# A fused Fourier-mixing and hard-swish kernel: weight conversions of the first block split into halves and reordered

## The chip, the cores and the metric

The kernel runs on one core of a Trainium2 chip. A core has five instruction streams that matter here: PE (TensorE, the matrix engine; "PEld" in the profile is its loading of weights, which overlaps its products), DVE (VectorE), ACT (ScalarE), POOL (GpSimd) and SP (SyncE, which here only issues DMAs). Each stream runs its instructions in the order in which they are written, and waits where a semaphore says that data or a buffer is not ready.

The metric is the device time of one execution in microseconds (us). Before the change the median of four runs is 2700.55 us.

## The reference

```python
def _attn_ref(x, filt_r, filt_i):          # x: 8 x 3008 x 256
    X = np.fft.rfft(x, axis=1)
    F = (filt_r + 1j * filt_i)[None, :, :]
    Y = X * F
    y = np.fft.irfft(Y, n=x.shape[1], axis=1)
    return y.astype(np.float32)
...
def _moe_ref(x, w_in, w_out):              # x: 24064 x 256, w_in: 256 x 2048, w_out: 2048 x 256
    h = x @ w_in
    relu6 = np.clip(h + 3.0, 0.0, 6.0)
    g = h * relu6 / 6.0
    return (g @ w_out).astype(np.float32)
```

A sequence of 3008 positions is filtered in the frequency domain, for 8 batches and 256 channels. The 24064 filtered tokens then go through a two-layer network with 2048 hidden units. The two weight matrices come in as 64-bit floats.

## The kernel before

**Blocks and steps.** The network is computed in 47 blocks of 512 tokens. A block takes 8 steps, one for each 256 of the 2048 hidden units (`NP` = 8). With `items` the program counts steps through all blocks: step 8k + p works on block k and hidden part p. In a step PE computes the "up" product (tokens times `w_in[p]`), ACT and DVE make the hard-swish of it, and in the following step PE computes the "down" product (hidden units times `w_out[p]`). Block 0 does this plainly (`plain_up`, L658; `plain_down`, L669): 512-wide products into two PSUM tiles `al` and `be`, then for each of them a `relu` on ACT (L616) and a `hswish` on DVE (L621). `al` can be written again when L621 has read it. From block 1 on (step 8), the products are done with fewer multiplications in a Strassen-like scheme (`up_1` to `up_5`, L571, and `down`, L647), which needs sums of weight blocks beside the weights themselves. These are made once by POOL (`w_sums`, L299): four for each of the 16 weight tiles, three early ones and a "late" one that overwrites a weight block which block 0 still needs.

**The Fourier work** runs between these steps. A function `at(step, fn, ...)` puts a call into a plan; calls of `a_unit`, `b_unit`, `bi_unit` and `n_unit` run early in their step, between the up and the down product, all others run at its end. In the first ten steps the plan has the following. `n_unit` turns transformed data into the tokens of block 1 and 2 (PE L525, ACT L531), after which `t_sums` makes token sums on POOL (L564). `a_unit(1, c)` is the first transform of batch 1, for chunk c in step c + 2: products into two PSUM banks (PE L385), each evicted by ACT (L388). For later batches the second bank goes through DVE (`a_sums`). `z_store` writes the result to DRAM, `x_load` fetches the next chunk, `table_load` the filter tables `ft0` and `ft1`, `t4_load` inputs of `n_unit`, `t2_load` reads the stored chunks back for `b_unit` (PE L437). For batch 1 all of these are issued by SP.

**The weights.** Each of the 16 weight tiles (up 0, down 0, up 1, down 1, ..., up 7, down 7) is loaded as raw 64-bit words (`w_load`, L260) and converted to 32 bits on DVE by seven instructions (`w_conv`, L275 to L293). ACT makes one operand, the magnitude of the upper word (`w_abs`, L266). The first four tiles are converted before block 0. The other twelve are converted by `convert_one` at the end of steps 0, 1, 1, 2, 2, 3, 3, 4, 4, 5, 5, 6, in the order up 2, down 2, up 3, down 3 and so on. `load_bits` asks for the next tile once the tile two places earlier in the same kind of buffer has been converted, so the order on SP's queue depends on where it is called. The sums on POOL are planned from step 6: first the early ones of up 7 and down 7, then stage p in step p + 6.

Of the kernel before, what the change touches and what calls it, by code (L numbers as in the profile page):

```python
# [38 lines left out]
NB = HC // XC  # L39
# [6 lines left out]
NP = DFF // 256  # L46
# [90 lines left out]
def kernel(  # L137
# [9 lines left out]
    nc = tc.nc  # L147
# [47 lines left out]
    st = {}  # L195
# [35 lines left out]

    NCONV = 16

    def w_part(i):
        p = i // 2
        if i % 2 == 0:
            cols = ts(p, 256)
            src = moe_w_in[:, cols].bitcast(I32)
            return src.rearrange("(a p) d -> p a d", p=P), w_in[p][:, 0:4, :].rearrange("p (a j) m -> p a (j m)", a=2)
        src = moe_w_out[ts(p, 2 * P), :].bitcast(I32)  # L240
        return src.rearrange("(a p) d -> p a d", p=P), w_out[p][:, 0:4, :].rearrange("p (a j) m -> p a (j m)", a=2)
# [21 lines left out]
    def w_abs(i):  # L263
        words = st["bits", i].rearrange("p (n two) -> p n two", two=2)
        st["high", i] = sp.tile([P, 512], FP32, name="s1")
        nc.scalar.activation(out=st["high", i], in_=words[:, :, 1].bitcast(FP32), func=AXT.Abs)  # L266


    def w_conv(i):
        words = st.pop(("bits", i)).rearrange("p (n two) -> p n two", two=2)  # L270
        lo, hi = words[:, :, 0], words[:, :, 1]
        big, rest = (yp.tile([P, 2, D], FP32, name="y").bitcast(I32).rearrange("p a n -> p (a n)") for j in range(2))
        v = nc.vector
        high = st.pop(("high", i), None)
        v.tensor_scalar(out=big, in0=hi, scalar1=3, scalar2=0x3FFFFFFF,  # L275
                        op0=ALU.logical_shift_left, op1=ALU.bitwise_and)
        v.scalar_tensor_tensor(out=big, in0=hi, scalar=top_c, in1=big,  # L277
                               op0=ALU.bitwise_and, op1=ALU.bitwise_or)
        v.tensor_scalar(out=rest, in0=big, scalar1=23, scalar2=23,
                        op0=ALU.logical_shift_right, op1=ALU.logical_shift_left)  # L280
        v.tensor_scalar(out=lo, in0=lo, scalar1=9, scalar2=0x3F800000,
                        op0=ALU.logical_shift_right, op1=ALU.bitwise_or)
        if high is None:
            v.tensor_scalar(out=hi, in0=hi, scalar1=1, scalar2=1,
                            op0=ALU.logical_shift_left, op1=ALU.logical_shift_right)
            high = hi.bitcast(FP32)
        rest, big = rest.bitcast(FP32), big.bitcast(FP32)
        v.scalar_tensor_tensor(out=rest, in0=lo.bitcast(FP32), scalar=1.0, in1=rest,  # L288
                               op0=ALU.subtract, op1=ALU.mult)
        v.scalar_tensor_tensor(out=rest, in0=rest, scalar=2.0 ** -20, in1=big, op0=ALU.mult, op1=ALU.add)  # L290

        two = lambda t: t.rearrange("p (a d) -> p a d", a=2)
        v.scalar_tensor_tensor(out=w_part(i)[1], in0=two(high), scalar=1.125 * 2.0 ** -15, in1=two(rest),  # L293
                               op0=ALU.is_ge, op1=ALU.mult)
# [74 lines left out]
    def bank(b):  # L369
        if b:  # L370
            return psF.tile([P, 512], FP32, name="psf", tag="f")
        st["bank"] = i = (st.get("bank", -1) + 1) % 4
        return psO.tile([P, 2, 2, P], FP32, name="po%d" % i).rearrange("p a u m -> p (a u m)")
# [4 lines left out]
    def a_unit(b, c):  # L378
        xc = xs[:, (b * NB + c) % 3, :, :]
        t = t1p.tile([P, XC // 2, 2, D], FP32, name="t1")  # L380
        ps = [bank(b).rearrange("p (j d) -> p j d", d=D) for h in range(2)]
        for j in range(2):
            for g in range(2):
                for h in range(2):
                    nc.tensor.matmul(ps[h][ts(g, 64), j, :], wa[ds(h * 64, NA), ds((c * XC + 2 * g + j) * 2 * KH, 64)],  # L385
                                     xc[ds(h * 64, NA), 2 * g + j, :], start=True, stop=True)
        for h in range(2 if b == 1 else 1):
            nc.scalar.activation(out=t[:, :, h, :], in_=ps[h], func=AXT.Copy)  # L388
        st["t1", b, c] = t, ps[1]


    def a_sums(b, c):
        t, ps = st["t1", b, c]
        nc.vector.tensor_tensor(out=t[:, :, 1, :], in0=t[:, :, 0, :], in1=ps, op=ALU.subtract)
        nc.vector.tensor_tensor(out=t[:, :, 0, :], in0=t[:, :, 0, :], in1=ps, op=ALU.add)  # L395

# [100 lines left out]
    for b in range(B):  # L497
        j = 0
        while j < HC:
            n = 1 if b == 0 and j == NJ else min(NJ, HC - j)  # L500
# [229 lines left out]


    EARLY = (a_unit, b_unit, bi_unit, n_unit)

    def at(step, fn, *a):
        plan.setdefault((step, fn in EARLY), []).append((fn, a))

    with tc.manual_schedule():
# [16 lines left out]
        def load_bits(most):  # L754
            nonlocal loaded
            while loaded < most and w_before(loaded) < done:
                w_load(loaded, nc.sync)
                loaded += 1

        def convert(n):  # L760
            nonlocal done
            for i in range(n):
                w_conv(done)
                done += 1


        def convert_one():
            nonlocal done
            w_abs(done)
            w_conv(done)  # L770
            done += 1
            load_bits(NCONV)

# [2 lines left out]
        ps = psU.tile([P, 512], FP32, name="al")  # L776
# [12 lines left out]
        for j in range(0, HC, 4):  # L789
            a0_unit(j)  # L790
            keep_warm({4: 2, 12: 2, 20: 1}.get(j, 0))
            convert(j == 4)
# [34 lines left out]
        for c in range(2):  # L827
            x_load(1, c)
            load_bits(7 + c)
        w_abs(3)  # L830
        convert(3)

        def wai_load():
# [3 lines left out]
        at(0, bi_unit, 0, NU - 2)  # L837
        at(0, g_store, 0, NU - 2)

        for i, s in enumerate((0, 1, 1, 2, 2, 3, 3, 4, 4, 5, 5, 6)):  # L840
            at(s, convert_one)

        for i in range(2):
            at(6, w_sums, 2 * NP - 2 + i, False)
        for p in range(NP):
            for i in range(2):
                if p < NP - 1:
                    at(p + 6, w_sums, 2 * p + i, False)
                at(p + 6, w_sums, 2 * p + i, True)

        at(0, wai_load)
        at(2, x_load, 1, 2)
# [31 lines left out]
        def places(n):  # L884
            if n == 1:
                return (list(range(2, NB + 2)), [12, 13, 15, 18, 19, 20, 22, 23, 26, 27, 28, 30],
                        [14, 15, 16, 19, 21, 22, 24, 25, 27, 29, 30, 31], [16, 21, 24, 29, 31, 32])
            k = first[n] * NP
            a_at = [k - 7 * NP + i for i in (2, 4, 7, 9, 11, 13, 14, 15)]
            f_at, y_at, bi_at = ([k - (5 - 2 * r) * NP + i for r in range(2) for i in p]  # L890
                                 for p in ((2, 3, 6, 7, 12, 13), (4, 5, 10, 11, 14, 15), (8, 14, 17)))
            return a_at, f_at, y_at, bi_at

        prev = None
        for n in range(1, B):
            a_at, f_at, y_at, bi_at = places(n)
            for c, s in enumerate(a_at):
                at(s, a_unit, n, c)
                if n > 1:
                    at(s, a_sums, n, c)  # L900
                at(s, z_store, n, c, nc.sync if n == 1 else nc.gpsimd)
                if c >= 3:
                    at(max(a_at[c - 3], s - 6), x_load, n, c)
                elif n > 1:
                    at(max(prev[c + NB - 3], s - 6), x_load, n, c)
            for c in range(NT):
                s = f_at[2 * (c - TB) + (n == 1)] + 1 if c >= TB else a_at[-1] + 1
                at(s, t2_load, n, c)
                s = f_at[2 * (c - FB) + 1] + 1 if c >= FB else a_at[-1 if n > 1 else 3] + 1
                at(s, table_load, n, c)  # L910
            for i in range(NU):
                if i % 2 == 0 or n == 1:
                    at(f_at[i], b_unit, n, i)
                if i % 2 == 0:
                    at(bi_at[i // 2], bi_unit, n, i)
                    at(bi_at[i // 2], g_store, n, i)
                at(y_at[i], y_unit, n, i)
            for i in range(NU):
                at(f_at[i], f_unit, n, i)
            prev = a_at  # L920
# [4 lines left out]
        for i in range(len(items) + 1):  # L925
            up = i < len(items)
            k, p = items[min(i, len(items) - 1)]
# [54 lines left out]
        k, v, add = NBLK - 1, nc.vector.tensor_tensor, ALU.add  # L982
# [37 lines left out]
```

## Time and profile before

| | us |
|---|---|
| median of 4 runs | 2700.55 (2699.74 to 2701.25) |
| the profiled execution, as timed | 2700.58 |
| its span, first to last instruction | 2698.8 |
| granted TensorE clock | 0.999 |

| engine | busy, us | share of the span |
|---|---|---|
| PE | 2675.0 | 99% |
| PEld | 2365.8 | 88% |
| DVE | 2020.6 | 75% |
| ACT | 1306.4 | 48% |
| POOL | 365.5 | 14% |

In the profile an instruction is named by its line (L277 is line 277 of the kernel before), its engine, its operation, and by the tile that it writes and the tiles that it reads. Times start with the span. A bracket such as [1.17 <-DVE g L621] says that the engine stood idle for 1.17 us before this instruction, and whose end let it go on. Matrix products are pipelined and their ends are modelled, so starts are safer to read than durations.

The starts of the eight steps of block 0 and of step 8 on PE are 67.56, 72.21, 79.20, 87.31, 97.22, 107.86, 117.41, 127.05 and 135.26 us. The steps differ in the Fourier work that they hold: `bi_unit` in step 0, nothing in step 1, `a_unit` from step 2 on, `n_unit` in steps 3 and 4.

### The profile page before, as it was taken

The numbers are of one execution on the slowest core, as the hardware profiler recorded it, in microseconds if no ns is written. First come the engines' busy times: TensorE is split into PE (matmuls) and PEld (weight loads), VectorE is DVE, ScalarE is ACT, GpSimd is POOL, SyncE is SP. The second block draws the span as 40 slices with busy tenths as digits, with TensorE's granted clock in tenths as the row PEclk, the third lists the DMA queues.
The fourth block names the chain that finished last, engine by engine and source line by source line (L and its number), as shares of the span: only waits on it lengthen the run. The fifth ranks groups of instructions, "written<-read, shape, count | busy, mean of one in ns | idle before, by whom it ended". The sixth has DMA issues, their size and how long they took to land.

```text
span 2698.8 us, 48891 instructions
## 1 busy us (share of the span) xinstructions
PE 2675.0 (99%) x18846; PEld 2365.8 (88%) x18846; DVE 2020.6 (75%) x3503; ACT 1306.4 (48%) x2614; POOL 365.5 (14%) x598
## 2 busy tenths in 40 slices
PE   8999999999999999999999999999999999999998
PEld 6588898888988888888888888988888888899997
DVE  7968867787678776787767877677776778766665
ACT  3444444445444444454544545445444454445443
POOL 2141011001210012101121011211112111000000
PEclk9999999999999999999999999999999999999999
DMA  9732133211332113311133111331113321110000
GB/s 238 219 93 70 46 89 99 70 35 42 92 99 63 36 47 95 99 55 37 49 95 96 55 39 52 89 96 55 39 55 89 93 59 36 42 31 18 18 9 17
DMA packets 106598, 185.89 MB, mean 69 GB/s; under 512 B 23609, under 2 KB 66297, under 8 KB 106049
## 3 DMA queue, kind: packets, MB, share of 16 engines
q1 hardware_dynamic: 88607, 138.05, 17.8%
q0 software_dynamic: 17152, 44.22, 6.2%
q8 instruction: 149, 2.44, 0.4%
q14 instruction: 84, 0.69, 0.1%
q10 hardware_dynamic: 606, 0.49, 0.1%
HBM read 110.74 MB, written 71.93 MB: 68 GB/s over the span
## 4 chain that ended last, share of the span: by engine, by line
PE 96%; DVE 2%; DMA 1%; SPq 0%; ACT 0%; issue 0%; POOL 0%; POOLq 0%; DVEq 0%; ACTq 0%
PE po L647 43%; PE al L571 24%; PE be L571 18%; PE psn L525 4%; PE psf L472 2%; PE psf L385 2%; PE psf L428 1%; PE po L352 1%; DMA g_tmp<-t 0%; PE psf L437 0%; DVE g L621 0%; PE po L437 0%; PE al L780 0%; DVE y L277 0%; DVE y L288 0%
## 5 line engine op out<-in xcount | busy, mean ns | idle before, releaser
L647 PEld LDWEIGHTS po<-w_all,g 128*128 128x128 f32 x10304 | 1363.4, 191 | 149.2 <-issue 41.4
L647 PE MATMUL po<-w_all,g 128*128 128x128 f32 x10304 | 1403.1, 276 | 0.6 <-DVE g L621 0.6
L616 ACT ACTIVATE r<-h,half_c 128x512 f32<-128x512 f32 x736 | 531.1, 722 | 328.9 <-DVE h L597 316.8
L621 DVE SCALAR_TENSOR_TENSOR g<-r,h 128x512 f32<-128x512 f32 x736 | 508.1, 690 | 206.3 <-ACT r L616 191.5
L571 PE MATMUL al<-xt,w_all 128*128 128x256 f32 x2208 | 660.1, 381 | 1.2 <-DVE h L602 0.6
L571 PE MATMUL be<-xn,w_all 128*128 128x256 f32 x1472 | 437.8, 379 | 0.0
L597 DVE TENSOR_TENSOR h<-be,s 128x512 f32<-128x512 f32 x368 | 254.3, 691 | 219.5 <-PE be L571 208.2
L571 PEld LDWEIGHTS al<-xt,w_all 128*128 128x128 f32 x2208 | 335.3, 192 | 2.5 <-DVE h L602 1.2
L571 PEld LDWEIGHTS be<-xn,w_all 128*128 128x128 f32 x1472 | 279.7, 190 | 37.9
L611 ACT ACTIVATE h<-al 128x256 f32<-128x256 f32 x368 | 141.0, 383 | 344.0 <-PE al L571 344.0
L602 DVE TENSOR_TENSOR h<-al,s 128x256 f32<-128x256 f32 x368 | 156.2, 424 | 166.7 <-PE al L571 165.6
L629 DVE TENSOR_TENSOR g<-g 128x512 f32<-128x512 f32 x368 | 256.0, 696 | 12.6
L592 ACT ACTIVATE s<-al 128x256 f32<-128x256 f32 x368 | 141.2, 384 | 205.7 <-PE al L571 203.6
L583 ACT ACTIVATE s<-be 128x256 f32<-128x256 f32 x368 | 141.1, 383 | 176.6 <-PE be L571 176.6
L571 PE MATMUL al<-xn,w_all 128*128 128x256 f32 x736 | 219.9, 381 | 0.5 <-ACT h L611 0.5
L571 PE MATMUL be<-xt,w_all 128*128 128x256 f32 x736 | 218.9, 379 | 0.0
L631 DVE TENSOR_TENSOR g<-g 128x256 f32<-128x256 f32 x368 | 169.9, 462 | 12.5
L582 ACT ACTIVATE s<-al 128x256 f32<-128x256 f32 x368 | 141.1, 383 | 71.3 <-PE al L571 71.2
L628 DVE TENSOR_TENSOR g<-g 128x256 f32<-128x256 f32 x368 | 157.2, 427 | 12.6
L571 PEld LDWEIGHTS be<-xt,w_all 128*128 128x128 f32 x736 | 139.8, 190 | 18.9
L402 POOL DMA_DIRECT2D z_tmp<-t x192 | 95.2, 502 | 417.4 <-DVE t L395 399.1
L492 POOL DMA_DIRECT2D g_tmp<-t x84 | 52.7, 632 | 584.3 <-ACT t L475 584.3
(139 smaller groups left out, 1811.5 us busy)
## 6 DMA issues: line engine op xcount, KB each, us to landing
g_tmp<-t POOLq DMA_DIRECT2D x96, 256.0 KB, 3.7
t<-g_tmp SPq DMA_DIRECT2D x188, 120.0 KB
t<-z_tmp SPq DMA_DIRECT2D x42, 512.0 KB
z_tmp<-t POOLq DMA_DIRECT2D x192, 96.0 KB, 3.2
out_dram<-o SPq DMA_DIRECT2D x321, 47.0 KB
xs<-in_x_dram SPq DMA_DIRECT2D x112, 128.0 KB
ft<-in_filt_r_dram SPq DMA_DIRECT2D x168, 64.0 KB
ft<-in_filt_i_dram SPq DMA_DIRECT2D x168, 64.0 KB
```

The costliest lines, as they stand in the source:

```text
L571: nc.tensor.matmul(ps, w_in[p][:, w, :], x, start=start, stop=stop, skip_group_check=True)
L582: nc.scalar.activation(out=s[:, 0, :], in_=al, func=AXT.Copy)
L583: nc.scalar.activation(out=s5, in_=be[:, 1, :], func=AXT.Copy)
L592: nc.scalar.activation(out=s[:, 1, :], in_=al, func=AXT.Copy)
L597: nc.vector.tensor_tensor(out=st["h"][0].rearrange("p (a n) -> p a n", a=2), in0=be, in1=s, op=ALU.add)
L602: nc.vector.tensor_tensor(out=st["h"][1][:, 256:512], in0=al, in1=s5, op=ALU.add)
L616: nc.scalar.activation(out=r, in_=st["h"][i], func=AXT.Relu, bias=half_c, scale=1.0 / 6.0)
L621: nc.vector.scalar_tensor_tensor(out=st["g", k, p][:, o:o + 2, :].rearrange("p a n -> p (a n)"), in0=st["r", i], scalar=1.0, in1=st["h"][i ...
L628: v.tensor_tensor(out=g[:, G1, :], in0=g[:, G3, :], in1=g[:, G22, :], op=ALU.add)
L629: v.tensor_tensor(out=g[:, G3:G2 + 1:2, :], in0=g[:, G3:G1 + 1, :], in1=g[:, G11:G11 + 1, :].broadcast_to([P, 2, 256]), op=ALU.subtract)
L631: v.tensor_tensor(out=g[:, G4, :], in0=g[:, G12, :], in1=g[:, G2, :], op=ALU.subtract)
L647: nc.tensor.matmul(st["po", k][bank][:, part, u, :], g[:, a, ts(u, P)], w_out[p][:, w, :], start=(p == 0 and n in OPENS and u == 0), stop= ...
```

## The change

The 16 weight tiles are taken in another order, set by `PART`: from the fifth on up 2, up 3, down 2, up 4, down 3, up 5, down 4, up 6, down 5, up 7, down 6, down 7. `w_conv` is cut in two: `w_conv` makes the first four instructions, `w_conv_2` the last three. The plan places 24 halves: 3, 3, 3, 4, 4, 3, 2, 2 in steps 0 to 7. A first half brings `w_abs` with it, a second half `load_bits`.

For batch 1 the second bank of chunks 6 and 7 (steps 8 and 9) is evicted by DVE instead of ACT, in `a_sums`, at the end of the step.

POOL's sums begin with the early ones of down 6 in step 6; stage p then comes in step p + 6, the late one of down 6 in step 12, and the sums of stage 7 in step 13.

```diff
+    PART = (0, 1, 2, 3, 4, 6, 5, 8, 7, 10, 9, 12, 11, 14, 13, 15)
+
     def w_part(i):
+        i = PART[i]
         p = i // 2
...
-        high = st.pop(("high", i), None)
+        st["conv", i] = big, rest, lo, hi
         v.tensor_scalar(out=big, in0=hi, scalar1=3, scalar2=0x3FFFFFFF,
                         op0=ALU.logical_shift_left, op1=ALU.bitwise_and)
...
         v.tensor_scalar(out=lo, in0=lo, scalar1=9, scalar2=0x3F800000,
                         op0=ALU.logical_shift_right, op1=ALU.bitwise_or)
+
+    def w_conv_2(i):
+        big, rest, lo, hi = st.pop(("conv", i))
+        v = nc.vector
+        high = st.pop(("high", i), None)
...
-        for h in range(2 if b == 1 else 1):
+        for h in range(2 if b == 1 and c < NB - 2 else 1):
             nc.scalar.activation(out=t[:, :, h, :], in_=ps[h], func=AXT.Copy)
...
     def a_sums(b, c):
         t, ps = st["t1", b, c]
+        if b == 1:
+            if c >= NB - 2:
+                nc.vector.tensor_copy(out=t[:, :, 1, :], in_=ps)
+            return
...
-        def convert_one():
+        def convert_half(second):
             nonlocal done
-            w_abs(done)
-            w_conv(done)
+            if not second:
+                w_abs(done)
+                w_conv(done)
+                return
+            w_conv_2(done)
             done += 1
             load_bits(NCONV)
...
-        for i, s in enumerate((0, 1, 1, 2, 2, 3, 3, 4, 4, 5, 5, 6)):
-            at(s, convert_one)
-
-        for i in range(2):
-            at(6, w_sums, 2 * NP - 2 + i, False)
-        for p in range(NP):
-            for i in range(2):
-                if p < NP - 1:
-                    at(p + 6, w_sums, 2 * p + i, False)
-                at(p + 6, w_sums, 2 * p + i, True)
+        half = 0
+        for s, n in enumerate((3, 3, 3, 4, 4, 3, 2, 2)):
+            for i in range(n):
+                at(s, convert_half, half % 2)
+                half += 1
+
+        order = [2 * NP - 3] + [i for i in range(2 * NP) if i != 2 * NP - 3]
+        for i in order:
+            at((6 + i // 2) if i != order[0] else 6, w_sums, i, False)
+            if i != order[0]:
+                at(6 + i // 2, w_sums, i, True)
+        at(6 + order[0] // 2, w_sums, order[0], True)
...
-                if n > 1:
-                    at(s, a_sums, n, c)
+                at(s, a_sums, n, c)
```

## Prediction

> **What bounds the kernel now.** I began with the busy table: TensorE is busy for 2675.0 of 2698.8 us, so no edit that leaves its work alone can give more than the 23.8 us in which it stands. The table of busy time by stretches says where those are (span from:to, its length, then PE's busy time with its number of instructions, and the other engines').
>
> ```profile
> PE 2675.0 (99%) x18846; PEld 2365.8 (88%) x18846; DVE 2020.6 (75%) x3503; ACT 1306.4 (48%) x2614; POOL 365.5 (14%) x598
> ...
> 87.10:97.00 9.90, 9.82 (x51) 6.44 (x50) 9.42 (x17) 4.27 (x8) 1.18 (x1) 1.00 0.99 266
> 97.00:107.00 10.00, 9.92 (x52) 6.44 (x50) 9.52 (x15) 3.62 (x7) 2.49 (x3) 1.00 0.15 40
> 107.00:120.00 13.00, 11.27 (x48) 6.16 (x47) 12.41 (x24) 3.88 (x7) 0.00 (x0) 1.00 0.71 219
> 120.00:140.00 20.00, 18.19 (x104) 11.54 (x103) 13.00 (x22) 8.17 (x16) 8.87 (x20) 1.00 0.68 192
> 140.00:150.00 10.00, 9.47 (x62) 7.55 (x61) 4.78 (x8) 5.73 (x11) 9.29 (x19) 1.00 0.25 68
> ...
> 400.00:2400.00 2000.00, 2000.00 (x14420) 1782.21 (x14419) 1523.56 (x2644) 986.27 (x1988) 261.38 (x428) 1.00 0.23 65
> ```
>
> The middle 2000 us have no hole. The first block with its next step, 107 to 150 us, has 1.73 + 1.81 + 0.53 = 4.07 us, and there DVE is the full engine (12.41 of 13.00). All that the change touches lies here, so I read PE's order of work (start, duration, and in brackets the idle time with its releaser):
>
> ```profile
> 97.22 1.88 PE L658 MATMUL al<-xn,w_all 128*128 128x512 f32 x4
> ...
> 107.86 1.98 PE L658 MATMUL al<-xn,w_all 128*128 128x512 f32 x4 [0.57 <-DVE g L621]
> 109.69 1.88 PE L658 MATMUL be<-xn,w_all 128*128 128x512 f32 x4
> 111.50 1.09 PE L385 MATMUL psf<-xs,wa 47*64 47x256 f32 x16
> 112.52 3.72 PE L669 MATMUL po<-w_all,g 128*128 128x256 f32 x16
> 117.41 1.98 PE L658 MATMUL al<-xn,w_all 128*128 128x512 f32 x4 [1.17 <-DVE g L621]
> 127.05 1.98 PE L658 MATMUL al<-xn,w_all 128*128 128x512 f32 x4 [1.26 <-DVE g L621]
> 135.26 0.59 PE L571 MATMUL al<-xn,w_all 128*128 128x256 f32 x2
> 139.35 0.67 PE L571 MATMUL al<-xt,w_all 128*128 128x256 f32 x2 [0.55 <-ACT s L592]
> ```
>
> Each step of the block begins with L658 into `al`, and `al` is free only when DVE's L621 has read it. DVE's own order shows why that is late: a step there is two conversions and then the pair of L621.
>
> ```profile
> 107.13 0.68 DVE L621 SCALAR_TENSOR_TENSOR g<-r,al 128x512 f32<-128x512 f32 x1
> 107.72 0.68 DVE L621 SCALAR_TENSOR_TENSOR g<-r,be 128x512 f32<-128x512 f32 x1
> 108.32 0.42 DVE L275 TENSOR_SCALAR y<-bits 128x512 int32<-128x512 int32 x1
> 110.37 0.69 DVE L288 SCALAR_TENSOR_TENSOR y<-bits,y 128x512 f32<-128x512 f32 x1
> 112.50 0.42 DVE L275 TENSOR_SCALAR y<-bits 128x512 int32<-128x512 int32 x1
> 116.67 0.68 DVE L621 SCALAR_TENSOR_TENSOR g<-r,al 128x512 f32<-128x512 f32 x1
> ```
>
> From these rows: a conversion is 112.50 - 108.32 = 4.18 us, its first half (to L288) 2.05, its second 2.13; a pair of L621 1.19. So DVE needs 2 x 4.18 + 1.19 = 9.55 us a step. PE moves on 0.74 us after the first L621 starts (117.41 - 116.67). What PE itself needs I take from steps that did not wait: 79.20 to 87.31 is 8.11 us with `a_unit`, 87.31 to 97.22 is 9.91 with `a_unit` and five products of `n_unit`. Steps 4 to 7 (97.22 to 135.26) took 38.04 and need 9.91 + 3 x 8.11 = 34.24: DVE costs **3.80 us** here.
>
> **Part 1, the halves moved to later steps.** DVE's instructions stay the same twelve conversions; only their places differ (halves 3, 3, 3, 4, 4, 3, 2, 2 in steps 0 to 7, instead of whole conversions 1, 2, 2, 2, 2, 2, 1). I lay them out with the durations above. DVE's first L621 of steps 1 to 7 stands at:
> - step 1: 72.63 + 4.18 + 2.04 = 78.85, where before it stood at 76.81. PE's step 2 starts at 79.59 instead of 79.20, and a start after a wait has cost 0.10 more (109.69 - 107.86 = 1.83 against 1.72): a **loss of 0.49**.
> - step 2: 80.04 + 6.31 = 86.35, allowing PE 87.09; PE is there at 79.59 + 0.10 + 8.11 = 87.80. No wait, 0.7 in hand.
> - step 3: 93.76 allows 94.50; PE comes at 97.71. Step 4: 94.95 + four halves 8.36 = 103.31, and 1.3 more because the conversion at 101.61 ran 5.5 instead of 4.18 us beside POOL's L564 (102.65 to 105.14), whose place hardly moves: 104.6 allows 105.4; PE comes at 107.62.
> - step 5: 105.8 + 8.36 = 114.2 allows 114.9; PE comes at 115.73: 0.8 in hand, the thinnest place.
> - step 6: 115.4 + 6.31 = 121.7 allows 122.4; PE comes at 123.84. Step 7: L621 waits only for its own `be`.
> PE reaches step 8 at 123.84 + 8.11 = 131.95 instead of 135.26: **gain 3.31**, which is 3.80 - 0.49.
>
> Are the weights there? Up 3 is done by 82.2 and used at 87.8; down 2 done 86.4, used 94; down 5 done 117.5, used 120.2; down 6 done 122.9 + 4.18 = 127.0, used 128.5; down 7 done 128.9 + 4.18 = 133.1, used 136.0. The waits are covered by 1.5 us or more; without that cover each costs what it is late.
>
> The loads: `load_bits` now follows the second half, so up 4 to down 7 are asked for when L288 of two tiles earlier has run. For the ninth conversion that is 106.6 instead of 105.75; it took 4.4 us then (issue 105.75, ACT's L266 released at 110.12), so 111.0 against a first half at 112.1. On ACT, the two `relu` of step 5 stand behind that L266 and run by about 113, before 114.2. SP queues its z_store of chunk 1 ahead of that load instead of behind it, which is earlier. The last load goes out at 120.25 instead of 120.66; behind it on SP stand t4_load, z_store of chunk 3, x_load of chunk 6, both tables (`ft`) and z_store of chunk 5, so this queue gains only 0.4 us where PE gains 3.3. Its users then: x of chunk 6 had come by 129.98, PE wants it at 132.8; z_store of chunk 5 was issued by 141.0 (now 140.6) and must have landed for ACT's copy of chunk 7, before at 147.07, now at 143.2; t2_load, before at 162.89, comes some 1.9 earlier, and its product (PE L437 at 169.96, now 166.1) had about 3.5 us to spare and keeps about 1.6. All covered, less well than before.
>
> **Part 2, the second eviction of chunks 6 and 7 goes from ACT to DVE.** In step 8 ACT ran two L388 (137.84, 1.08 us together) ahead of L592, which let L571 go at 139.35 with 0.55 idle. One copy less puts L592 0.54 earlier: **gain 0.50** of the 0.55. Chunk 7 showed no such wait (PE L571 at 149.25 has no bracket): 0. On DVE a 128x512 copy out of PSUM took 0.69 (the one `t<-be` at 27.3), against 0.59 on ACT; DVE sat idle 3.55 us before its next L621 at 145.16 and 1.30 before that at 152.38, so 0.69 fits. Were that cover gone, L621 would come 0.7 late, and the down product after it. The banks are given back a little later, 142 instead of 139; the next `a_unit` wants them at 145.9 - 3.8 = 142.1 and that copy shifts too, to 138.5, so 0.
>
> **Part 3, POOL's order.** Its sums were gated by the last two conversions (up 7, then down 7) and ran on from 131.98; now they are gated by down 6 alone: from 127.1, with three sums of down 6 first. Sums of stage 0 are ready by 130.6, of use at 132.4. The number of sums is the same, 64 in steps 6 to 13. The price is that the conversion of down 7 and step 8 of DVE run beside POOL. By the rows: beside L299 an L629 took 0.83 against 0.69, an L621 0.91 against 0.69, while the L275 at 127.50 kept its 0.42; three or four instructions of this kind make 0.7 us, out of 2.9 in hand: cost 0, bound 0 to 0.7.
>
> The Trainium skill (SBUF — State Buffer, "Who interferes with whom") speaks against this part: it calls the pair of ports that VectorE and GpSimd share an exclusive lock, where the loser blocks for the whole instruction. By that rule every instruction of the conversion could wait for one sum of 0.49 us, seven of them 3.4 us, and down 7 would be late by 0.5, which makes the gain 3.3 instead of 3.8. The rows above show part of an instruction lost, not a whole one, and I go by the rows.
>
> **The sum.** 3.31 + 0.50 = 3.8 us off the profiled execution (2698.8 span, 2700.58 with what lies around it; the median of the four runs, 2700.55, is the same). After 150 us the order is unchanged and PE is full, so the shift is kept: 2700.55 - 3.8 = **2696.8 us**.
>
> **The rivals.**
> - A, the forecast: 0.72, own range 2696.1 to 2697.6.
> - B, SP's queue becomes the end of the shift: it gains 0.4 to 1.9 us, PE 3.8, and either z_store of chunk 5 or t2_load ends last. For it: the last load is anchored in DVE's order. Against it: 1.3 and 1.6 us to spare. Gain 1.9: 2698.7. Chance 0.12.
> - C, the lead taken in the block is paid for on DVE in steps 5 to 8 (POOL beside it, 0.8 us in hand at step 5): about 1 us back, 2697.8. Chance 0.05.
> - D, slower: a `relu` of step 5 behind L266, which waits for the ninth load. It decides from a landing at 112.2 on and costs one for one; it turns the sign when the load lands 3.8 us later still, at 116, that is 9.4 us after its issue against the 4.4 seen. Lasting two loads that way: 2702. Chance 0.06; over 0.2% in half of it.
> - E, more than the sum: steps 3 and 4 also held L385 up for 0.5 each behind ACT's L531, which I count as staying. With both gone and no loss in step 2, 5.3 us: 2695.2. Chance 0.05.
>
> **How the numbers follow.** 0.2% is 5.4 us, about what a measurement of this kernel tells from no change, and more than all of PE's idle time in the block. Faster by that: E's upper half and what no row here lets me see, 0.06; slower: half of D, 0.03; within: 0.91. The range 2695.8 to 2699.0 holds A, B and C, 0.89 of the chance if each were exact; allowing for their edges I take it as 8 in 10.
>
> **What would show it.** PE's L658 starts near 79.6, 87.8, 107.6, 115.7 and 123.8 without a bracket on DVE except the first, and L571 near 131.9; the gap before L571 in step 8 falls from 0.55 to under 0.2; POOL's sums run from about 127. Wrong if a bracket stays at the steps after 107, if ACT's L266 stands before a `relu` that DVE waits for, or if a gap appears at L437 near 166.

## The result and the profile after

The changed kernel takes 2697.45 us (median of 39 runs, 2696.71 to 2701.96); the kernel before, run beside it on the same chips, 2700.99 us (59 runs). The ratio is 0.9987 with a 95% interval of 0.9983 to 0.9992: 2.2 to 4.6 us less, 3.5 in the medians. The forecast was 2696.8 in a range of 2695.8 to 2699.0, and "within 0.2%" is what came. Eight of the 39 runs, and 11 of the 59 before, are longer than the others by about 3 us or more (most by 3 to 4); experiments 4 and 7 to 10 deal with these.

The profiled execution has a span of 2694.7 us (2696.45 with what lies around it) at a clock of 0.999. First its busy table:

```profile
PE 2674.3 (99%) x18846; PEld 2366.0 (88%) x18846; DVE 2022.6 (75%) x3505; ACT 1305.4 (48%) x2612; POOL 367.6 (14%) x598
```

PE's work is the same as before. DVE has the two copies that ACT lost. The table of busy time by stretches (from:to, length, then PE, PEld, DVE, ACT and POOL, each with its number of instructions, the granted clock, and the DMA share and rate):

```profile
97.00:107.00 10.00, 9.92 (x52) 6.53 (x51) 9.62 (x17) 3.92 (x7) 2.68 (x3) 1.00 0.49 155
107.00:120.00 13.00, 13.00 (x67) 7.15 (x66) 12.32 (x23) 5.46 (x9) 0.00 (x0) 1.00 0.50 161
120.00:140.00 20.00, 19.34 (x103) 13.60 (x101) 14.00 (x22) 8.30 (x17) 13.42 (x26) 1.00 0.68 189
140.00:150.00 10.00, 10.00 (x76) 8.69 (x77) 7.15 (x11) 5.00 (x10) 9.37 (x18) 1.00 0.19 48
```

The hole of 1.73 us between 107 and 120 is gone, though DVE is about as full there as before: it does the same work, but PE no longer waits for it. From 120 to 140, 1.81 us of idle time became 0.66. PE's order of work, with the idle time in front of an instruction and its releaser in brackets:

```profile
66.94 1.98 PE L670 MATMUL al<-xn,w_all 128*128 128x512 f32 x4 [0.34 <-ACT xn L567]
71.59 1.98 PE L670 MATMUL al<-xn,w_all 128*128 128x512 f32 x4
78.84 1.98 PE L670 MATMUL al<-xn,w_all 128*128 128x512 f32 x4
...
106.87 1.88 PE L670 MATMUL al<-xn,w_all 128*128 128x512 f32 x4
114.98 1.88 PE L670 MATMUL al<-xn,w_all 128*128 128x512 f32 x4
123.09 1.88 PE L670 MATMUL al<-xn,w_all 128*128 128x512 f32 x4
131.19 0.59 PE L583 MATMUL al<-xn,w_all 128*128 128x256 f32 x2
...
134.87 0.67 PE L583 MATMUL al<-xt,w_all 128*128 128x256 f32 x2
...
139.96 0.70 PE L583 MATMUL al<-xn,w_all 128*128 128x256 f32 x2 [0.53 <-ACT h L623]
...
165.49 1.03 PE L449 MATMUL psf<-t,wf 128*128 128x256 f32 x4
```

The up products now stand in L670 (before L658) and L583 (before L571). The brackets on DVE at 107.86, 117.41 and 127.05 have no successor, nor has the 0.55 on ACT inside step 8. The 0.53 ahead of step 9 was there before, too (at 144.43). The one wait that the prediction put in, at step 2, shows in the start: step 1 takes 7.25 us (78.84 - 71.59), where it took 6.99 (79.20 - 72.21).

The block begins at 66.94 here and at 67.56 before. The program ahead of it is the same but for which weight tile a load fetches, and in seven profiles (these two and experiments 1, 2, 3, 5 and 6) the block begins anywhere from 66.94 to 68.02, as the loads in front of it land. So I count from the block's start. Step 8 comes 64.25 us after it (131.19 - 66.94), before 67.70: **3.45 us gained in the block**. Step 8 itself takes 8.77 (139.96 - 131.19), before 9.17: **0.40 us**. Step 9 starts 4.47 earlier in all (0.62 of it by the earlier start of the block), and PE L449 at 165.49 is 4.47 earlier as well, the last product of the kernel 4.44: the lead is kept.

### The profile page after: what moved, and what is told of

Its sections match the earlier page's. It is cut to its first block, busy times and chain, and to the rows that moved or that the text cites. A ratio compares the mean times of both kernels' runs of the same rounds, so it can differ in the third digit from the quotient of the medians.

```text
span 2694.7 us, 48891 instructions
## 1 busy us (share of the span) xinstructions
PE 2674.3 (99%) x18846; PEld 2366.0 (88%) x18846; DVE 2022.6 (75%) x3505; ACT 1305.4 (48%) x2612; POOL 367.6 (14%) x598
## 3 DMA queue, kind: packets, MB, share of 16 engines
q8 instruction: 149, 2.44, 0.4%
## 4 chain that ended last, share of the span: by engine, by line
PE 98%; DVE 1%; DMA 0%; ACT 0%; issue 0%; POOL 0%; SPq 0%; POOLq 0%; DVEq 0%
PE po L659 43%; PE al L583 24%; PE be L583 18%; PE psn L537 4%; PE psf L393 2%; PE psf L484 2%; PE psf L440 1%; PE po L681 1%; PE po L360 1%; PE al L670 0%; PE be L670 0%; PE po L449 0%; PE psf L449 0%; PE al L796 0%; DMA g_tmp<-t 0%
## 5 line engine op out<-in xcount | busy, mean ns | idle before, releaser
L633 DVE SCALAR_TENSOR_TENSOR g<-r,h 128x512 f32<-128x512 f32 x736 | 508.5, 691 | 204.9 <-ACT r L628 190.0
L583 PE MATMUL al<-xt,w_all 128*128 128x256 f32 x2208 | 660.1, 381 | 0.7 <-DVE h L614 0.6
L583 PE MATMUL be<-xn,w_all 128*128 128x256 f32 x1472 | 437.8, 379 | 0.0
L609 DVE TENSOR_TENSOR h<-be,s 128x512 f32<-128x512 f32 x368 | 254.3, 691 | 215.1 <-PE be L583 210.1
L583 PEld LDWEIGHTS al<-xt,w_all 128*128 128x128 f32 x2208 | 335.3, 192 | 2.1 <-DVE h L614 1.2
L583 PEld LDWEIGHTS be<-xn,w_all 128*128 128x128 f32 x1472 | 279.7, 190 | 38.0
L604 ACT ACTIVATE s<-al 128x256 f32<-128x256 f32 x368 | 141.2, 384 | 206.2 <-PE al L583 204.0
L583 PE MATMUL al<-xn,w_all 128*128 128x256 f32 x736 | 219.9, 381 | 0.5 <-ACT h L623 0.5
L583 PE MATMUL be<-xt,w_all 128*128 128x256 f32 x736 | 218.9, 379 | 0.0
L583 PEld LDWEIGHTS be<-xt,w_all 128*128 128x128 f32 x736 | 139.8, 190 | 18.9
```

The source lines that it names most:

```text
L583: nc.tensor.matmul(ps, w_in[p][:, w, :], x, start=start, stop=stop, skip_group_check=True)
L604: nc.scalar.activation(out=s[:, 1, :], in_=al, func=AXT.Copy)
L609: nc.vector.tensor_tensor(out=st["h"][0].rearrange("p (a n) -> p a n", a=2), in0=be, in1=s, op=ALU.add)
L633: nc.vector.scalar_tensor_tensor(out=st["g", k, p][:, o:o + 2, :].rearrange("p a n -> p (a n)"), in0=st["r", i], scalar=1.0, in1=st["h"][i ...
```

## The experiments

Each experiment's kernel was run 11 times beside the kernel before. "Block" is step 0 to step 8 on PE in the profile, "step 8" is step 8 to step 9. The medians of 2 and 4 hold many of the long runs (5 and 7 of 11), so the parts of the change are read from the profiles.

| | median, us | ratio (95%) | block | step 8 |
|---|---|---|---|---|
| before | 2700.99 | | 67.70 | 9.17 |
| changed | 2697.45 | 0.9987 (0.9983 to 0.9992) | 64.25 | 8.77 |
| 1: copy back on ACT | 2697.80 | 0.9987 (0.9979 to 0.9996) | 64.26 | 9.17 |
| 2: only the copy on DVE | 2702.02 | 1.0004 (0.9995 to 1.0012) | 67.69 | 8.76 |
| 3: POOL's sums after the last tile | 2702.20 | 1.0004 (0.9996 to 1.0013) | 64.26 | 11.66 |
| 4: whole conversions | 2700.33 | 0.9990 (0.9981 to 0.9999) | 65.48 | 8.77 |
| 5: old order of tiles | 2701.25 | 0.9998 (0.9989 to 1.0007) | 67.37 | 8.76 |
| 6: POOL's sums ungated | 2699.78 | 0.9994 (0.9985 to 1.0003) | 66.30 | 8.76 |
| 7: 4 with ten products in the gap | 2698.11 | 0.9986 (0.9977 to 0.9995) | 63.90 | 8.76 |
| 8: before with ten products in the gap | 2701.82 | 1.0000 (0.9992 to 1.0009) | 67.68 | 9.17 |
| 9: 4 with three products | 2697.17 | 0.9983 (0.9974 to 0.9992) | 63.89 | 8.76 |
| 10: changed with three products | 2697.20 | 0.9982 (0.9973 to 0.9991) | 64.26 | 8.76 |

### 1 and 2: the copy by itself

Experiment 1 is the changed kernel with the copies of chunks 6 and 7 back on ACT:

```diff
-        for h in range(2 if b == 1 and c < NB - 2 else 1):
+        for h in range(2 if b == 1 else 1):
...
-            if c >= NB - 2:
-                nc.vector.tensor_copy(out=t[:, :, 1, :], in_=ps)
             return
```

> The changed kernel with the second bank of chunks 6 and 7 evicted by ACT again. My theory: only step 8 loses, by the 0.4 to 0.5 us that L604 (then behind two copies) holds up_3's product; the steps of block 0 keep their starts, so 2.9 to 3.1 us of the 3.5 stay against the kernel before (about 2698.0). Rival, that the eviction carries the gain: back to about 2700.5.

Experiment 2 is the kernel before with that part of the change alone.

> The kernel before with the eviction of chunks 6 and 7 alone on DVE. My theory: 0.4 to 0.5 us faster than before, from the gap at 139.35 alone, with the waits of L658 at steps 5 to 7 unchanged (sum 3.0 us). Rival, that DVE being late makes its copy cost something: 0 or up to 0.7 slower.

PE's order of work in experiment 1:

```profile
136.36 0.67 PE L581 MATMUL al<-xt,w_all 128*128 128x256 f32 x2 [0.55 <-ACT s L602]
141.45 0.70 PE L581 MATMUL al<-xn,w_all 128*128 128x256 f32 x2 [0.53 <-ACT h L621]
```

The old bracket of 0.55 behind ACT is back, and step 8 takes 9.17 again, while the block keeps its 64.26. In experiment 2 the block's waits stay:

```profile
108.23 1.98 PE L662 MATMUL al<-xn,w_all 128*128 128x512 f32 x4 [0.57 <-DVE g L625]
117.77 1.98 PE L662 MATMUL al<-xn,w_all 128*128 128x512 f32 x4 [1.16 <-DVE g L625]
127.41 1.98 PE L662 MATMUL al<-xn,w_all 128*128 128x512 f32 x4 [1.26 <-DVE g L625]
144.38 0.70 PE L575 MATMUL al<-xn,w_all 128*128 128x256 f32 x2 [0.53 <-ACT h L615]
```

and step 8 takes 8.76 (144.38 - 135.62). So the two parts add up and don't touch each other: 0.40 for the copy, 3.45 for the rest. The runs can't show 0.4 us; the profiles can, because steps that nothing was changed in repeat to 0.02 us from one kernel to the next.

### 3 and 6: where POOL's sums may begin

In experiment 3 the sums wait for the last conversion, as before the change, with the halves as changed:

```diff
-        order = [2 * NP - 3] + [i for i in range(2 * NP) if i != 2 * NP - 3]
...
+        at(6, w_sums, 2 * NP - 2, False)
+        at(7, w_sums, 2 * NP - 1, False)
+        for p in range(NP):
+            for i in range(2):
+                if p < NP - 1:
+                    at(max(p + 6, 7), w_sums, 2 * p + i, False)
+                at(max(p + 6, 7), w_sums, 2 * p + i, True)
```

> The changed kernel with POOL's sums gated as before, by up 7 and then by down 7, the last conversion (now in step 7). My theory: the conversion of down 7 runs alone and ends near 132.2, its three sums take 1.7 us, and the first sum of stage 0 is there near 134.4, where PE wants it at 131.6: a stall of 2.8 us in step 8, so most of the gain is gone (2699.9 to 2700.5). Rival, that POOL's order is of no weight, as the prediction priced it: no stall, 2697.0 to 2697.5, perhaps 0.1 better because the conversion of down 7 has no company.

PE and POOL in experiment 3:

```profile
135.28 0.70 PE L583 MATMUL be<-xt,w_all 128*128 128x256 f32 x2 [2.63 <-POOL w_all L307]
```

```profile
133.30 23.32 POOL L307 TENSOR_TENSOR w_all<-w_all 128x128 f32<-128x128 f32 x43 [10.63 <-DVE w_all L301]
```

The block is as quick as in the changed kernel, and step 8 then stands for 2.63 us in its second product, because the sums of stage 0 are not there. Moving the conversions later without moving POOL's gate gives most of the gain back one step on. The profile was of the quickest of the 11 runs; these spread from 2700.35 to 2706.59, and their median lies 1.7 us above the upper end of what was expected. The four longest (2702.93 and more) had a mean granted clock of 0.997 or less, the others 0.998, so a lower clock has a part in it; no profile shows where.

Experiment 6 goes to the other side: sums from step 6, with nothing of down 6 in front of them to hold them back.

```diff
-        order = [2 * NP - 3] + [i for i in range(2 * NP) if i != 2 * NP - 3]
...
+        for i in range(2 * NP):
+            at(6 + i // 2, w_sums, i, False)
+            at(6 + i // 2, w_sums, i, True)
```

> The changed kernel with POOL's sums from step 6 on without the early ones of down 6 in front, so that stage 0 is gated by nothing near and its sums start near 105, beside four conversions instead of one. Measured in the changed kernel: the conversion of down 7 beside POOL took 5.3 us instead of 4.18. My theory: each of the conversions of steps 4 to 6 costs 1.1 us more; DVE had 1.9 us in hand at step 6, so L670 waits by 0.5 to 1.5 us at steps 6 to 7: 0.5 to 1.5 us slower than the changed kernel. Rival with whole instructions blocked (0.49 us for each of seven): 3 us and more slower. Rival that the place of the sums is free: no difference.

POOL in the changed kernel, then POOL, DVE and PE in experiment 6:

```profile
125.48 25.12 POOL L307 TENSOR_TENSOR w_all<-w_all 128x128 f32<-128x128 f32 x43 [20.42 <-DMA z_tmp<-t]
```

```profile
106.02 28.54 POOL L307 TENSOR_TENSOR w_all<-w_all 128x128 f32<-128x128 f32 x40
```

```profile
107.40 0.68 DVE L278 TENSOR_SCALAR y<-bits 128x512 int32<-128x512 int32 x1
...
112.64 0.69 DVE L278 TENSOR_SCALAR y<-bits 128x512 int32<-128x512 int32 x1
```

```profile
124.98 1.98 PE L670 MATMUL al<-xn,w_all 128*128 128x512 f32 x4 [0.56 <-DVE g L633]
130.69 3.72 PE L681 MATMUL po<-w_all,g 128*128 128x256 f32 x16 [0.98 <-DVE w_all L301]
```

POOL starts at 106.02 instead of 125.48. (The bracket at 125.48 names a DMA, but the conversion of down 6 had ended at 125.33, 0.15 us earlier; in experiment 1 the same bracket names DVE's L301.) The conversions of steps 4 to 7 now run beside it: 112.64 - 107.40 = 5.24 us from one first half to the next, where the changed kernel has 110.42 - 106.25 = 4.17. DVE falls behind; PE waits for `al` ahead of step 7 and, inside it, for the tile of down 6 (the second was not foreseen). From step 1 to step 8 PE takes 61.65 us instead of 59.60, 2.05 more, above the 0.5 to 1.5 expected. POOL pays as well: a sum takes 0.71 us on average here (28.54 for 40), 0.58 in the changed kernel (25.12 for 43). The gate on down 6 stands between two costs. Counted from the block's start POOL begins at 58.5 us in the changed kernel; at 38.1 (experiment 6) PE loses 2.05, at 65.5 (experiment 3) 2.89 (11.66 - 8.77).

### 5: the old order of tiles

`PART = tuple(range(16))`, all else as changed.

> The changed kernel with the tiles in their old order (up 2, down 2, up 3, down 3, ...), halves and their steps as changed. My theory: the up tile of a step is now the last to be converted, so up 5 is done about 0.5 us after PE wants it, up 6 about 2 us and up 7 only near 126.5 on the changed kernel's clock, where its step 7 began at 123.1: L670 of step 7 starts 3.3 to 3.6 us late and step 8 stays late: 2700.5 to 2701.0, all of the gain gone. Rival, that only the steps of the halves count and weights are always there: no difference to the changed kernel (2697.4).

```profile
116.11 1.98 PE L670 MATMUL al<-xn,w_all 128*128 128x512 f32 x4 [0.58 <-DVE w_all L301]
...
126.49 1.99 PE L670 MATMUL al<-xn,w_all 128*128 128x512 f32 x4 [2.00 <-DVE w_all L301]
```

These are the starts of PE's steps 6 and 7. The releaser is no longer L633 (the hard-swish) but L301, the last instruction of a conversion: `al` is free, but the weights of the up product are not there. The block takes 67.37, 3.12 more than changed, which is all but 0.33 of the block's gain; step 7 starts 3.01 later than there, where 3.3 to 3.6 were expected. Later halves are only worth something if the up tile is converted ahead of the down tile that PE wants a step after it.

### 4: is it the halves?

The four halves that stood alone at the ends of steps 0, 2, 3 and 4 move to the step after, so that every step holds whole conversions; the order of tiles and POOL's gate stay as changed:

```diff
-        for s, n in enumerate((3, 3, 3, 4, 4, 3, 2, 2)):
+        for s, n in enumerate((2, 4, 2, 4, 4, 4, 2, 2)):
```

> The changed kernel with whole conversions: 2, 4, 2, 4, 4, 4, 2, 2 halves in steps 0 to 7, so none is cut by a pair of L633; order of tiles, eviction and sums as changed. My theory: it is the later place and the order of the tiles that count, not the cut; step 2 loses nothing, and steps 3 to 8 still find al free (DVE allows 87.1 at step 3, where PE comes at 87.3): 0.3 to 0.5 us faster than the changed kernel (2697.0). Rival, that the cut is needed to level DVE's load: L670 waits again in steps 3 to 6, 1 us or more slower than the changed kernel.

The runs fell into two groups: four at 2696.3 to 2697.8, seven at 2699.7 to 2701.1, so the median, 2700.33, is not the 2697.0 expected. The profile was of the second. PE ahead of the block and at the starts of steps 0, 1 and 8:

```profile
65.25 3.72 PE L565 MATMUL psn<-wai,t 128*128 128x94 f32 x20 [1.81 <-DMA xs<-in_x_dram]
...
69.76 3.58 PE L670 MATMUL al<-xn,w_all 128*128 128x512 f32 x4
...
76.00 1.98 PE L670 MATMUL al<-xn,w_all 128*128 128x512 f32 x4
...
135.24 0.59 PE L583 MATMUL al<-xn,w_all 128*128 128x256 f32 x2
```

The first two took 2.44 and 1.98 us in the changed kernel. The table by stretches shows a lower clock there (the third number from the right is the granted clock):

```profile
60.00:66.10 6.10, 4.29 (x23) 2.88 (x21) 5.69 (x12) 0.00 (x0) 0.42 (x1) 1.00 0.58 174
66.10:73.00 6.90, 6.90 (x23) 4.99 (x22) 4.59 (x8) 2.07 (x5) 0.71 (x2) 0.51 1.03 347
73.00:80.00 7.00, 7.00 (x24) 2.82 (x23) 4.64 (x9) 3.99 (x7) 1.30 (x2) 1.00 0.47 121
```

After a gap of 1.81 the clock is half for 6.83 us (from 66.17, 0.92 after PE had taken up its work, to 73.00), which costs about 3.4 us (half of it; 1.59 of that falls on step 0, 6.24 us instead of 4.65), and from 76.00 on all is as ever. From there, step 1, to step 8 it takes 135.24 - 76.00 = 59.24 us, where the changed kernel takes 59.60, and no step waits for DVE. So the cut into halves is not what pays: with whole conversions in the new places the block is 0.36 us *shorter*, which is the loss that the third half in step 0 causes at step 2.

### 7 to 10: filling the gap

To see whether the two groups come from that gap, PE is given something to do in it: products of zeros into a tile that the block overwrites, in front of the last products ahead of the block. They compute nothing that is used.

```diff
+        ps_w = psU.tile([P, 512], FP32, name="be")
+        for i in range(10):
+            nc.tensor.matmul(ps_w[:, 0:P], zero[:, P:2 * P], zero[:, 0:P], start=True, stop=True)
         n_first()
```

Experiment 7 has ten of them in the kernel of experiment 4, experiment 8 ten in the kernel before; 9 and 10 have three, in the kernel of experiment 4 and in the changed one.

> The run with whole conversions, and ten 128-column products of zeros on PE (1.1 us) in its wait for t4 ahead of block 0. In the profile of the whole conversions PE stood 1.81 us there, and the granted clock was 0.5 for the next 6.83 us; the other profiles had gaps up to 1.50 and no drop. My theory: this is what lifts some executions of every kernel here by about 3.5 us; with the gap filled none is left, and the median is 2696.5 to 2697.0, spread under 2. Rival, that the drop has nothing to do with this gap: half of the executions stay near 2700.5.

> The kernel before with the same ten products in the same place. By the theory of the gap: the executions at 2703.5 to 2705 vanish, the median stays at 2700.5 to 2700.9, since most of its executions had no drop. Rival, that PE loses what the products take: 2701.5.

> Whole conversions as before in this study, with three products of zeros in the wait ahead of block 0 instead of ten (ten ran for 2.26 us, longer than the 1.2 to 1.8 us of the gap, and cost about 1 us). My theory: 0.7 us of filling leaves a gap of 0.5 to 1.1 us, short enough that no execution meets the lower clock, and nothing is delayed: median 2696.7 to 2697.1, none above 2698.5. Rival: the gap that counts is not this one, or 0.7 is too little: some executions near 2700.5 remain.

> The changed kernel with the same three products. My theory: 0.3 to 0.4 us slower than the run with whole conversions beside it, by the wait at step 2 alone; median 2697.1 to 2697.4, none above 2698.5. Rival, that the cut is worth its place in some way that one profile does not show: equal or faster than whole conversions.

None of these 44 runs is long, while the kernel before, run beside them, had long ones both times (11 of 33, then 4 of 20): experiment 7 spans 2697.39 to 2698.72, 8 spans 2701.24 to 2702.14 (the 11 long ones beside it lay at 2703.7 to 2705.3), 9 spans 2696.43 to 2698.01, 10 spans 2696.34 to 2697.84. Ten products take 2.26 us, twice what was expected and longer than the gap, so 7 and 8 lose about 1 us against runs that are not long; three are short enough. PE in experiment 9 (the profile counts two records for each of these products):

```profile
63.73 0.86 PE L843 MATMUL be<-r 128*128 128x128 f32 x6
65.15 2.44 PE L565 MATMUL psn<-wai,t 128*128 128x94 f32 x20 [0.56 <-issue]
```

The medians of 9 and 10 are 0.3 us under the changed kernel's, and the lowest of this study; without the long runs they equal its main group, so what the products buy is the missing tail. Whole conversions against halves is 59.24 against 59.61 from step 1 to step 8 in these two profiles, the same 0.37 as above, but the runs (2697.17 against 2697.20) don't resolve it.

## Why the prediction was right

**The layout of DVE's order held.** Relative to the block's start the prediction put PE's steps 2, 5, 6, 7 and 8 at 12.03, 40.06, 48.17, 56.28 and 64.39; they came at 11.90, 39.93, 48.04, 56.15 and 64.25. The constant 0.13 is from step 2: its wait moved it by 0.26 (7.25 us for step 1 against 6.99) and made step 2 itself 0.10 longer, 0.36 instead of the 0.49 in the sum. Experiments 4 and 9 show that loss from the other side: without the third half in step 0 it is not there. The 3.31 of part 1 was 3.45. Had the loss of step 2 been read as avoidable, whole conversions in the new places would have been the version to propose.

**The slack was mis-sized, harmlessly.** I called step 5 to 6 "the thinnest place" with 0.8 us in hand, because a conversion beside POOL's token sums (`t_sums`) was given 1.3 us more, as in the trace before. What it cost, and what POOL's weight sums cost the last conversion, is in DVE's order in the changed kernel:

```profile
104.50 1.11 DVE L298 SCALAR_TENSOR_TENSOR y<-y 128x512 f32<-128x512 f32 x1
...
106.25 0.42 DVE L278 TENSOR_SCALAR y<-bits 128x512 int32<-128x512 int32 x1
...
109.81 0.69 DVE L301 SCALAR_TENSOR_TENSOR w_all<-s,y 128x512 f32<-128x512 f32 x1
110.42 0.42 DVE L278 TENSOR_SCALAR y<-bits 128x512 int32<-128x512 int32 x1
...
112.34 0.70 DVE L633 SCALAR_TENSOR_TENSOR g<-r,al 128x512 f32<-128x512 f32 x1
...
125.72 0.69 DVE L633 SCALAR_TENSOR_TENSOR g<-r,al 128x512 f32<-128x512 f32 x1 [0.39 <-ACT r L628]
...
128.05 0.72 DVE L278 TENSOR_SCALAR y<-bits 128x512 int32<-128x512 int32 x1
128.80 0.83 DVE L280 SCALAR_TENSOR_TENSOR y<-bits,top_c,y 128x512 int32<-128x512 int32 x1
129.66 0.57 DVE L282 TENSOR_SCALAR y<-y 128x512 int32<-128x512 int32 x1
130.15 0.68 DVE L284 TENSOR_SCALAR bits<-bits 128x512 int32<-128x512 int32 x1
130.86 0.82 DVE L296 SCALAR_TENSOR_TENSOR y<-bits,y 128x512 f32<-128x512 f32 x1
131.72 0.83 DVE L298 SCALAR_TENSOR_TENSOR y<-y 128x512 f32<-128x512 f32 x1
132.65 0.76 DVE L301 SCALAR_TENSOR_TENSOR w_all<-s,y 128x512 f32<-128x512 f32 x1
134.84 0.69 DVE L609 TENSOR_TENSOR h<-be,s 128x512 f32<-128x512 f32 x1 [1.43 <-PE be L583]
```

Beside the three token sums from 102.39 on, one instruction, L298 at 104.50, took 1.11 instead of 0.69: 0.42 us, not 1.3. In the trace before three instructions of a conversion stood beside them; now the pair of L633 came to stand there (102.56 and 103.16), and both kept their 0.68. The L633 at 112.34 allowed PE 113.08 (0.74 after its start), and PE came at 114.98: 1.9 us in hand.

**Part 3 cost nothing on PE, but more on DVE than its bound.** The conversion of down 7, 128.05 to 132.65, has its last start 4.60 after its first; for an earlier one, alone, these starts were 106.25 and 109.81, 3.56 apart. That is 1.04 us, above my 0 to 0.7: I took three or four instructions as hit, and all seven were, by 0.07 to 0.30 each. The L275 that kept its 0.42 beside POOL was not the rule: here the same operation (L278) took 0.72. The tile was ready at 133.41 (132.65 + 0.76) and its down product began at 135.38, so 1.97 of cover hid it. The Trainium skill (SBUF — State Buffer, "Who interferes with whom") would have had an instruction wait for the whole of another; the 3.4 us worked out from it did not come, here or in the conversion of experiment 6 above (5.24 against 4.17). The conversion lost a quarter, not four fifths.

**Part 2** was given 0.50 of the 0.55 and brought 0.40; experiments 1 and 2 have it in both directions. The term took half of the pair's 1.08 us for the second copy. ACT's starts show less: from the pair to L592 it was 0.97 (137.84 to 138.81), from the one copy to the same instruction, now L604, 0.56 (133.78 to 134.34), so the second copy was worth 0.41. **The rivals:** B, SP's queue, did not end last: PE L449 at 165.49 has no bracket. C, a payback on DVE in steps 5 to 8, is in the rows above, but under cover. D, the `relu` behind the ninth load, did not occur: ACT's L269 does stand in front of the first `relu` of step 5, but it ran at 108.25, the `relu` at 108.85, as its product ended (106.87 + 1.88 = 108.75), and DVE's L633 began 3.5 us behind it. E's 5.3 us did not come; 0.36 of it, the loss of step 2, is to be had.

**The sum.** 3.8 us were forecast, 3.45 + 0.40 = 3.85 are in the profile, 3.5 between the medians. The 0.35 between them is less than the interval of the ratio can tell (2.2 to 4.6 us). That the sum lies within 0.05 is in part luck: part 1 came 0.14 higher than its term and part 2 0.10 lower. Of the 0.65 by which 2697.45 lies above 2696.8, 0.44 is the starting point: the forecast counts from 2700.55, the median of four runs, where 59 runs have 2700.99.

## What to carry to other kernels

Where one engine feeds another through a strict order, write down the feeder's instructions with their durations from the trace and see which of them stand in front of a release that the other waits for: the gain here is twelve conversions in another order, with nothing saved. Three places had to move together (the conversions, the order of the tiles, POOL's gate); without the second or the third, 3.1 or 2.9 us of the gain were lost again (the second and the third without the first were not run). And before cutting work into smaller pieces, try moving the whole pieces: the cut cost 0.36 us and bought nothing.

## What the runs showed of the hardware that was not expected

**A gap of under 2 us can be followed by half the TensorE clock.** In the profile of experiment 4, 1.81 us without a product were followed by 6.83 us at half clock, about 3.4 us lost. Gaps of 1.21 to 1.64 at the same place, in the profiles of the changed kernel, the kernel before and experiments 1, 2, 3, 5 and 6, were followed by none. Neither were two longer ones elsewhere: the 2.00 ahead of step 7 in experiment 5 and the 2.63 inside step 8 in experiment 3, where the granted clock stayed at 1.00. So the length of the gap alone does not decide it. Filling the gap with three products (0.86 us together) removed the long runs: of experiment 4's kernel 7 of 11 were long, of experiment 9's none. That the long runs of the kernel before and of the changed one are the same event is inferred: from their size (mostly 3 to 4 us); from the granted clock, whose mean over the run is 0.997 in all eight long runs of the changed kernel and 0.998 or 0.999 in its 31 others; and from experiments 8 and 10, where long runs are missing (11 in 59 and 8 in 39 without the products). No profile caught one. For experiment 10 by itself, 11 runs are few: experiment 6, without any products, had no long run in 11 either. The Trainium skill (TensorE: Matmul & The Clock Gate, "Why this matters for your kernels") advises against idle gaps of more than about 3 us; here one of 1.81 was followed by the drop once, while 2.00 and 2.63 passed without it. What decides beside the length stays open, with one profile that shows the drop.

**POOL's sums slow every instruction of a weight conversion on DVE**, also those with one input: `L278` 0.72 against 0.42, `L280` 0.83 against 0.75, `L284` 0.68 against 0.42, `L298` 0.83 against 0.69. Over a conversion it is about 1.05 us of 4.17, in the changed kernel once and in experiment 6 from one conversion to the next. It is not so each time (in experiment 6 the L278 at 131.75 kept 0.43), and it does not hold for instructions that read a PSUM tile: beside the same sums L633 on `al` at 125.72 and L609 on `be` at 134.84 took 0.69, as they do alone.
